# Attention and expert layers on one core: the scores of two key tiles merged in PSUM by a predicated copy before the bias is added

## The chip, the cores and the metric

The program runs on one core of one Trainium2 chip. The metric is the time of one execution on the device in microseconds (us). TensorE (PE) multiplies matrices and loads its weights through a queue of its own (PEld); VectorE (DVE), ScalarE (ACT) and GpSimd (POOL) do the rest; SyncE (SP) issues the loads and stores. PE writes its products to PSUM, six banks of which this kernel shares as `b`.

## The reference

```python
def _attn_ref(q, k, v):                      # 4 batches, 8 heads, 576 positions, 64 deep
    scores = scale * np.matmul(q, k.transpose(0, 1, 3, 2))
    rel = pos[:, None] - pos[None, :]
    bias = slopes[:, None, None] * (-np.abs(rel))[None, :, :]
    mask = (rel >= 0) & (rel < 128)
    scores = np.where(mask, scores + bias[None], -1000000000.0)
    attn = np.exp(scores - np.max(scores, axis=-1, keepdims=True))
    attn = attn / (np.sum(attn, axis=-1, keepdims=True) + 1e-09)
    return np.matmul(attn, v)

def _moe_ref(x, domain_probs, w1, w2):       # 2304 tokens, 512 wide, 4 experts, 1024 hidden
    for e in range(E):
        h = np.maximum(x @ w1[e], 0.0)
        out += p[:, e:e + 1] * (h @ w2[e])
```

A query sees itself and the 127 positions before it. So a tile of 128 queries needs two tiles of keys, its own and the one before, and of each pair of columns at the same offset exactly one is in the window: the own key where its offset is not above the query's, the earlier key where it is.

## The kernel before, in words

All arithmetic is 32-bit: a value that goes to PE is split into a high and a low part (tiles `kh`, `kl`, `w1h`, `w1l` and so on), and three products stand for one. The 2304 tokens are 18 tiles of 128 in seven blocks (`BLOCKS`): three of 256 tokens and four of 384. Attention for a block must be done before the expert layers (L923 first layer, L1111 second, L1001 a seven-product form for pairs of blocks) can use it. Attention is cut into units: one tile of 128 queries and one pair of heads. Block 0 (`plain`) has eight units and runs before anything else; block 1, also eight units, and the rest run among the expert products.

A planner (`Plan`) sets the order. Each piece of work is an `op` with the engines that may do it, a cost for each, a due time, the data that it reads and writes and the buffers that it holds; `Plan.order` goes through time, gives each op an engine and a buffer by these costs, and emits all instructions in that order. So a changed cost moves unrelated work too.

A unit (`unit`, L493) goes like this. PE writes the scores of both heads into one bank, up to 256 columns a head (L510 for block 0, L519 else). DVE adds the bias and takes the row's extreme (`least`, L555, one instruction a head). ACT takes exponentials with their sum (L573); the sum's reciprocal (L604) scales them (L612 on DVE or L620 on ACT); PE transposes them (L638); ACT or DVE split the result into high and low (L311, L313, L323) and PE multiplies with the values (L709). `pk` is the number of earlier keys that the tile has (0, 64 or 128: a sequence of 576 is four and a half tiles), `edge` is set where a sequence ends inside the tile.

The bias tile holds 256 columns a head: the same 128 numbers are loaded twice (L1178) and masked on POOL, one half for keys after the query, one for keys before (`seen`, L1164). From block 2 on (`FOLD`, L533) the two halves are folded after the bias: a minimum on DVE (L587) over the two 128-column halves, so that exponentials, scaling and transposes work on 128 columns. The transposed, split result is then parted again into own and earlier keys by two selections on POOL (`side`, L662). Tiles with `pk` of 64 fill the missing half with a memset (L551), tiles with an edge take a copy of the bias with a part overwritten (L544, L547). Block 1 has no fold: all stages run on 256 columns, four transposes a unit, and nothing for POOL to select.

Of the kernel before, what the change touches and what calls it, by code (L numbers as in the profile page):

```python
# [202 lines left out]
FOLD = 2  # L203

# [24 lines left out]
def attention_moe(  # L229
# [66 lines left out]
    bias = sb.tile([P, H, 2 * P], F32, tag="bias", name="bias")  # L296
# [117 lines left out]

    groups = {}
# [77 lines left out]
    def unit(u):  # L493
# [5 lines left out]
        edge = edge if edge < P else 0  # L499
        bk, s, t = Buf("b"), Buf("acc" if g.plain else "s"), Buf("t")  # L500
        sv = lambda: s[:, : 4 * P].rearrange("p (h n) -> p h n", h=2) if s.tag == "acc" else s.place
# [31 lines left out]
        fold = pk > 0 and g.nb >= FOLD  # L533
        o2, n2 = (P, P) if fold else (o, n)
# [3 lines left out]
        bkey = [("bias", g.hp)] if pk else [("bias", g.hp, 1)]  # L538
        bv = lambda: bias[:, hs, :]
        if edge:  # L540
            bb = Buf("x")
            b2 = lambda: bb[:].rearrange("p (h n) -> p h n", h=2)
            plan.op(
                {POOL: 0.75}, lambda e: nc.gpsimd.tensor_copy(b2(), bias[:, hs, :]), d - 1, [*bkey, "scores"], [bb], port=(POOL,)  # L544
            )
            plan.op(
                {POOL: 0.3}, lambda e: nc.gpsimd.memset(b2()[edge:, :, : P + edge], NEG), d - 1, [], [bb], port=()  # L547
            )
            bv, bkey = b2, [bb]
# [22 lines left out]
        def exponents(h):  # L572
            return lambda e: nc.scalar.activation(  # L573
                sv()[:, h, o2:],
                sv()[:, h, o2:],
# [6 lines left out]
        for h in range(2):  # L582
            plan.op({DVE: 0.15 + n / 960}, least(h), d + 0.3, [*bkey, bk], [(s, h), (t, h)])
        if fold:
            plan.op(
                {DVE: dve(2 * P)},
                lambda e: nc.vector.tensor_tensor(out=sv()[:, :, P:], in0=sv()[:, :, P:], in1=sv()[:, :, :P], op=ALU.min),  # L587
                d + 0.35,
                [(t, 0), (t, 1)],
                both,  # L590
                port=(DVE,),
            )
        for h in range(2):
            plan.op({ACT: 0.29 + n2 * 0.00087}, exponents(h), d + 0.4, [(t, h)], [(s, h), (t, 2 + h)])
# [15 lines left out]
        def weights_(e):  # L610
            if e == DVE:
                nc.vector.tensor_tensor(  # L612
                    out=sv()[:, :, o2:],
                    in0=sv()[:, :, o2:],
                    in1=t[:, 4:6, None].to_broadcast([P, 2, n2]),
# [3 lines left out]
            for h in range(2):  # L619
                nc.scalar.activation(sv()[:, h, o2:], sv()[:, h, o2:], AF.Copy, scale=t[:, 4 + h : 5 + h])  # L620

        plan.op({DVE: dve(2 * n2), ACT: 0.4 + n2 * 0.00174}, weights_, d + 0.7, [(t, 4)], both, port=(DVE,))
# [10 lines left out]
        tp = lambda: bk2[:].rearrange("p (h n) -> p h n", h=2)  # L633

        def transposed(e):
            for h in range(2):
                for c in (P,) if fold else (0, P)[2 - w // P :]:
                    nc.tensor.transpose(tp()[:, h, c : c + P], sv()[:, h, c : c + P], ident)  # L638

        tm = 2 if fold else 2 * w // P  # L640
# [3 lines left out]
        if g.plain:  # L644
            for h in range(2):
                cast(
                    lambda h=h: g.pt[h][:, c0 : c0 + w],
                    lambda h=h: tp()[:, h, 2 * P - w :],
# [6 lines left out]
        elif fold:  # L655
            hl = lambda: s[:].rearrange("p a b -> p (a b)").rearrange("p (x h n) -> p x h n", x=2, h=2)
            part = lambda x: hl()[:, x].bitcast(F32R)
            cast(lambda: part(0), lambda: tp()[:, :, P:], 2 * P, d + 0.9, [bk2], both, False)
            minus(lambda: part(1), lambda: tp()[:, :, P:], lambda: part(0), 2 * P, d + 1.0, [bk2], both, False)
# [14 lines left out]
        else:  # L674
            part = lambda x: pt[:, x, :, c0 : c0 + w]
            cast(lambda: part(0), lambda: tp()[:, :, 2 * P - w :], 2 * w, d + 0.9, [bk2], [(g.pt[0], i)], False)
            minus(
                lambda: part(1),
                lambda: tp()[:, :, 2 * P - w :],
                lambda: part(0),  # L680
                2 * w,
                d + 1.0,
                [bk2],
                [(g.pt[0], i)],
                False,
            )
# [475 lines left out]
    def seen(part, after):  # L1162

        return lambda e: nc.gpsimd.affine_select(  # L1164
            out=part,
            in_=part,
            pattern=[[0, 2], [1, P] if after else [-1, P]],
            base=0,
            channel_multiplier=-1 if after else 1,
            compare_op=ALU.is_gt if after else ALU.is_ge,  # L1170
            fill=NEG,
        )

# [145 lines left out]
```

## Time and profile before

| | |
|---|---|
| Runs of the kernel before | 903.31, 903.73 and 905.81 us; median 903.73 us |
| Span of the profiled execution, first to last instruction | 902.9 us |
| PE busy | 889.0 us, 98% |
| PEld, DVE, ACT, POOL busy | 805.3, 710.7, 449.9 and 371.3 us |
| DMA | 96.18 MB, 107 GB/s on average, 246 GB/s in the first fortieth of the span |

The profile is one execution; no time of its own is given for it apart from its span, which is 0.4 us below the fastest of the three runs and 0.8 us below their median. A busy engine is one with an instruction in work; matmuls overlap, so the distance from one start to the next tells more than their durations. A line number is a line of the kernel before; a helper's line (L311, L313, L323) stands for many uses, which are told apart by tile.

### The profile page before, as it was taken

What the parts mean: (1) busy time and instruction counts of PE and PEld (TensorE: products, weight loads), DVE (VectorE), ACT (ScalarE), POOL (GpSimd) and SP (SyncE); (2) the same over time, 40 slices, a digit from 0 to 9 for tenths busy, and PEclk for the clock granted to TensorE, in tenths of its full rate; (3) what the DMA queues carried; (4) which work ended last, traced back from release to release, by engine and by line L of the source; (5) the groups of instructions that cost most, each with busy time, mean ns of one, the idle gap of its engine ahead of it and who ended that gap; (6) DMA issues with size and microseconds to landing.
All of it is one profiled execution on the core that took longest, in us unless ns stands there. A gap on an engine that the chain in (4) does not pass through costs nothing.

```text
span 902.9 us, 14383 instructions
## 1 busy us (share of the span) xinstructions
PE 889.0 (98%) x5108; PEld 805.3 (89%) x5108; DVE 710.7 (79%) x1476; ACT 449.9 (50%) x1145; POOL 371.3 (41%) x348
## 2 busy tenths in 40 slices
PE   7899999999999999999999999999999999999998
PEld 5798999999999988999999998899898989989997
DVE  4888888687899899887887997677976767677765
ACT  4987454455556566765553344344333434344340
POOL 2656345253434467776525673213622222122100
PEclk9999999999999999999999999999999999999999
DMA  9766444243444345633111121212222121212001
GB/s 246 236 210 213 134 151 141 56 140 101 135 143 130 105 158 170 210 127 114 47 48 47 47 94 48 94 48 94 100 89 68 49 92 47 94 47 93 25 1 70
DMA packets 39959, 96.18 MB, mean 107 GB/s; under 512 B 3792, under 2 KB 17488, under 8 KB 39888
## 3 DMA queue, kind: packets, MB, share of 16 engines
q1 hardware_dynamic: 39888, 95.28, 32.6%
q8 instruction: 40, 0.66, 0.3%
q14 instruction: 31, 0.25, 0.1%
HBM read 90.54 MB, written 4.72 MB: 105 GB/s over the span
## 4 chain that ended last, share of the span: by engine, by line
PE 91%; DVE 6%; DMA 1%; ACT 1%; issue 1%; POOL 0%; DVEq 0%; POOLq 0%; ACTq 0%
PE b L1111 41%; PE b L923 22%; PE b L1001 18%; PE av L709 4%; PE b L519 3%; PE b L638 2%; DMA k<-in_qk 1%; PE b L510 1%; DVE w1l L323 1%; DMA w1r<-in_w 1%; DVE w2l L323 1%; DVE acc L1129 1%; DVE s L555 0%; DVE vs L323 0%; DVE x L736 0%
## 5 line engine op out<-in xcount | busy, mean ns | idle before, releaser
L1129 DVE SCALAR_TENSOR_TENSOR acc<-b,prob,acc 128x512 f32<-128x512 f32 (+1 forms) x229 | 169.8, 743 | 68.3 <-PE b L1111 67.5
L1111 PE MATMUL b<-w2h,rh 128*128 128x512 f32 x440 | 174.2, 396 | 0.0
L1111 PE MATMUL b<-w2h,rl 128*128 128x512 f32 x440 | 172.6, 392 | 0.4 <-DVE rl L951 0.4
L1111 PE MATMUL b<-w2l,rh 128*128 128x512 f32 x440 | 172.9, 393 | 0.0
L923 PE MATMUL b<-xh,w1h 128*128 128x256 f32 (+1 forms) x528 | 160.6, 304 | 1.3 <-ACT t L568 1.3
L923 PE MATMUL b<-xl,w1h 128*128 128x256 f32 (+1 forms) x528 | 157.0, 297 | 1.3 <-DVE xl L323 1.3
L923 PE MATMUL b<-xh,w1l 128*128 128x256 f32 (+1 forms) x528 | 157.0, 297 | 0.0
L323 POOL TENSOR_TENSOR w2l<-w2r,w2h 128x512 fp32r<-128x512 f32 x48 | 70.2, 1466 | 129.9 <-ACT w2h L311 116.3
L662 POOL TENSOR_SCALAR_AFFINE_SELECT pt<-s 128x512 fp32r<-128x512 f32 x104 | 67.9, 677 | 101.4 <-DVE s L323 79.1
L923 PEld LDWEIGHTS b<-xl,w1h 128*128 128x128 f32 x528 | 100.2, 190 | 3.7 <-DVE xl L323 1.7
L923 PEld LDWEIGHTS b<-xh,w1h 128*128 128x128 f32 x528 | 100.3, 190 | 3.5 <-ACT t L568 1.5
L944 ACT ACTIVATE rh<-b 128x256 fp32r<-128x256 f32 (+1 forms) x132 | 53.7, 407 | 96.9 <-PE b L923 92.1
L923 PEld LDWEIGHTS b<-xh,w1l 128*128 128x128 f32 x528 | 100.0, 189 | 0.0
L1111 PEld LDWEIGHTS b<-w2h,rl 128*128 128x128 f32 x440 | 82.6, 188 | 18.9 <-DVE rl L951 0.8
L1111 PEld LDWEIGHTS b<-w2h,rh 128*128 128x128 f32 x440 | 83.0, 189 | 10.6
L1111 PEld LDWEIGHTS b<-w2l,rh 128*128 128x128 f32 x440 | 83.0, 189 | 10.2
L951 DVE SCALAR_TENSOR_TENSOR rl<-b,rh 128x256 fp32r<-128x256 f32 (+1 forms) x132 | 60.2, 456 | 30.2 <-ACT rh L944 29.0
L323 POOL TENSOR_TENSOR w1l<-w1r,w1h 128x512 fp32r<-128x512 f32 x45 | 64.1, 1430 | 41.5 <-ACT w1h L311 17.9
L573 ACT ACTIVATE s<-s,t 128x128 f32<-128x128 f32 (+1 forms) x128 | 52.0, 408 | 47.7 <-DVE s L587 42.8
L1035 ACT ACTIVATE xh<-b 128x384 fp32r<-128x384 f32 x46 | 22.6, 491 | 92.3 <-DVE b L1020 85.4
L311 ACT ACTIVATE w2h<-w2r 128x512 fp32r<-128x512 f32 x109 | 64.5, 621 | 5.5 <-PE b L1111 4.5
L323 DVE TENSOR_TENSOR w2l<-w2r,w2h 128x512 fp32r<-128x512 f32 x72 | 62.5, 881 | 0.3 <-ACT w2h L311 0.2
(157 smaller groups left out, 1967.8 us busy)
## 6 DMA issues: line engine op xcount, KB each, us to landing
w1r<-in_w SPq DMA_DIRECT2D x60, 512.0 KB, 4.2
w2r<-in_w SPq DMA_DIRECT2D x60, 512.0 KB, 3.5
q<-in_q SPq DMA_DIRECT2D x16, 384.0 KB, 3.4
k<-in_k SPq DMA_DIRECT2D x12, 512.0 KB, 3.9
k<-in_k SPq DMA_DIRECT2D x12, 384.0 KB, 3.7
out<-acc SPq DMA_DIRECT2D x17, 256.0 KB, 2.1
v<-in_v SPq DMA_DIRECT2D x12, 256.0 KB, 2.9
v<-in_v SPq DMA_DIRECT2D x12, 192.0 KB, 3.4
```

Of the source, the lines that this page charges most:

```text
L311: nc.scalar.activation(o(), i(), AF.Copy)
L323: by[e].tensor_tensor(out=o(), in0=a(), in1=f(b()), op=ALU.subtract)
L519: nc.tensor.matmul(sc()[:, h, :n], g.qs[:, h, u.q0 : u.q0 + P], m[:, h, u.k0 : u.k0 + n], start=m is g.kh, stop=m is g.kl,)
L573: return lambda e: nc.scalar.activation(sv()[:, h, o2:], sv()[:, h, o2:], AF.Exp, bias=t[:, h : h + 1], scale=-1.0, accum_out=t[:, 2 + h : ...
L662: return lambda e: nc.gpsimd.affine_select(out=pt[:, :, :, c0 + own * P : c0 + own * P + P], in_=hl(), pattern=[[0, 4], [1, P] if own else ...
L709: nc.tensor.matmul(g.av[h][:, q0 : q0 + m], v2, g.pt[h][:, c : c + m] if g.plain else pt[:, x, h, c : c + m], start=not g.started[h], stop ...
L923: nc.tensor.matmul(bk[:, :n], a[0][:, kt, fs], b[:, kt, cols], start=kt == 0 and i == 0, stop=kt == KT - 1 and i == 2,)
L944: lambda e: nc.scalar.activation(h[:, :n], bk[:, :n], AF.Relu),
L951: lambda e: nc.vector.scalar_tensor_tensor(out=lo[:, :n], in0=bk[:, :n], scalar=0.0, in1=f(h[:, :n]), op0=ALU.max, op1=ALU.subtract,),
L1001: nc.tensor.matmul(bank[:, :n], x(k), y(k), start=new and k == 0 and i == 0, stop=k == 1 and i == 2, skip_group_check=True,)
L1111: nc.tensor.matmul(bk[:, cs], a[:, ns], b[1][:, fi, cs], start=half != 1 and fi == 0 and j == 0, stop=half != 0 and fi == 1 and j == 2, sk ...
L1129: nc.vector.scalar_tensor_tensor(out=o, in0=i_, scalar=p, in1=o, op0=ALU.mult, op1=ALU.add)
```

## The change

`FOLD` goes. Every unit outside block 0 with earlier keys is folded, so block 1 too, and the fold moves ahead of the bias: a predicated copy on DVE writes the earlier tile's scores over the own tile's in PSUM wherever a constant mask `after` says that the key is later than the query. The bias is then 128 columns a head, loaded once and unmasked. Where a mask is still needed (block 0, tiles with `pk` below 128, edges) POOL makes a masked copy of the bias for that unit in a buffer `x`. `least` works on 128 columns a head; the minimum and the memset are gone. The stages behind it and the selections are those of the fold before.

```diff
-FOLD = 2
...
-    bias = sb.tile([P, H, 2 * P], F32, tag="bias", name="bias")
+    bias = sb.tile([P, H, P], F32, tag="bias", name="bias")
+    after = sb.tile([P, 2, P], F32, tag="after", name="after")
...
+        fold = not g.plain
...
-        fold = pk > 0 and g.nb >= FOLD
...
+        if g.plain:
+            if u.first:
+                g.bb = Buf("x")
...
+            if pk:
+                plan.op({POOL: 0.45}, seen(lambda: b2()[:, :, :P], bv, True), d - 1, [bkey], [(bb, 0)], port=(POOL,))
+            else:
+                plan.op({POOL: 0.45}, seen(lambda: b2()[:, :, P:], bv, False), d - 1, [bkey], [(bb, 1)], port=(POOL,))
...
+        elif edge or pk < P:
+            bb = Buf("x")
...
-        if 0 < pk < P:
-            plan.op({POOL: 0.3, DVE: 0.28}, lambda e: by[e].memset(sv()[:, :, :o], -NEG if fold else 0.0), d, ["scores"], both, port=())
+        if fold and pk:
+            plan.op(
+                {DVE: 0.1 + 2 * pk / 960},
+                lambda e: nc.vector.copy_predicated(sc()[:, :, P:n], after[:, :, o:].bitcast(mybir.dt.uint32), sc()[:, :, :pk]),
+                d + 0.25,
+                ["after"],
+                [bk],
+            )
+        m = P if fold else n
+        f0 = n - m
...
         def least(h):
             return lambda e: nc.vector.tensor_tensor_reduce(
-                out=sv()[:, h, o:],
-                in0=sc()[:, h, :n],
-                in1=bv()[:, h, o:],
+                out=sv()[:, h, -m:],
+                in0=sc()[:, h, f0:n],
+                in1=bv()[:, h, :],
...
-        if fold:
-            plan.op(
-                {DVE: dve(2 * P)},
-                lambda e: nc.vector.tensor_tensor(out=sv()[:, :, P:], in0=sv()[:, :, P:], in1=sv()[:, :, :P], op=ALU.min),
...
-        for i, due in ((1, -37), (0, -33)):
...
+        load(
+            lambda hs=hs: bias[:, hs, :],
+            lambda hs=hs: bfd[:, hs, :],
+            131072,
+            -37 + 6 * hp,
```

The planner orders the whole program anew. Three places of that order are shown.

The first is SP's queue behind the first load of the program, up to the third load of keys and queries for block 0 (`k_63` the second time; `k_63` and `k_64` are the two buffers of keys and queries). Before:

```order
L304 DMA bias<-in_bias 128x2x128
L304 DMA v_65<-in_v 128x256
L304 DMA ident<-in_ident 128x128
L304 DMA bias<-in_bias 128x2x128
L304 DMA k_64<-in_qk 64x1024
L304 DMA bias<-in_bias 128x2x128
L304 DMA v_66<-in_v 128x256
L304 DMA bias<-in_bias 128x2x128 x3
L304 DMA dp<-in_dp 128x72
L304 DMA k_63<-in_qk 64x1024
```

Changed:

```order
L303 DMA bias<-in_bias 128x256
L303 DMA v_65<-in_v 128x256
L303 DMA ident<-in_ident 128x128
L303 DMA k_64<-in_qk 64x1024
L303 DMA bias<-in_bias 128x256
L303 DMA v_66<-in_v 128x256
L303 DMA bias<-in_bias 128x256
L303 DMA dp<-in_dp 128x72
L303 DMA bias<-in_bias 128x256
L303 DMA w1r_91<-in_w 128x1024
L303 DMA q_61<-in_q 128x2x256
L303 DMA k_63<-in_qk 64x1024
```

Two loads of bias fewer stand ahead of the third `k` (four against six), and the first load of weights and one of `q` have moved ahead of it.

The second is DVE's queue at one unit of a later block (`s_75` and `s_76` hold the unit's scores, `b_` are PSUM banks, `ISA` is the instruction of `least` and its read of the extreme into `t_`). Before:

```order
L555 ISA s_75,t_83<-b_126,bias 128x256
L555 ISA t_83 128x1
L951 SCALAR_TENSOR_TENSOR rl_107<-b_124,rh_103 128x256
L555 ISA s_75,t_83<-b_126,bias 128x256
L555 ISA t_83 128x1
L313 CAST s_77<-b_121 128x256
L323 TENSOR_TENSOR s_77<-b_121,s_77 128x256
L587 TENSOR_TENSOR s_75<-s_75 128x2x128
```

Changed:

```order
L586 COPY_PREDICATED b_125<-after,b_125 128x2x128
L312 CAST s_75<-b_122 128x256
L595 ISA s_76,t_81<-b_125,bias 128x128
L595 ISA t_81 128x1
L322 TENSOR_TENSOR s_75<-b_122,s_75 128x256
L595 ISA s_76,t_81<-b_125,bias 128x128
L595 ISA t_81 128x1
```

The fold has moved from behind the two instructions of `least` to ahead of them, and these have half the columns.

The third is POOL's queue while block 1's units run. Before, it holds only splits of weights, keys, queries and values:

```order
L323 TENSOR_TENSOR qs_67<-q_61,qs_67 64x2x256
L323 TENSOR_TENSOR vs_73<-v_65,vs_73 128x3x128
L323 TENSOR_TENSOR w1l_97<-w1r_91,w1h_95 128x512
L323 TENSOR_TENSOR w2l_102<-w2r_94,w2h_100 128x512
L323 TENSOR_TENSOR kl_72<-k_64,kh_70 128x2x384
L323 TENSOR_TENSOR w1l_98<-w1r_92,w1h_96 128x512
L323 TENSOR_TENSOR w2l_101<-w2r_93,w2h_99 128x512 x2
```

Changed:

```order
L322 TENSOR_TENSOR qs_67<-q_61,qs_67 64x2x256
L322 TENSOR_TENSOR vs_74<-v_66,vs_74 128x3x128
L705 AFFINE_SELECT pt<-s_75 128x4x128 x2
L322 TENSOR_TENSOR w2l_101<-w2r_93,w2h_99 128x512
L705 AFFINE_SELECT pt<-s_76 128x4x128 x2
L322 TENSOR_TENSOR w2l_101<-w2r_93,w2h_99 128x512
L322 TENSOR_TENSOR qs_68<-q_62,qs_68 64x2x256
L705 AFFINE_SELECT pt<-s_77 128x4x128 x2
L705 AFFINE_SELECT pt<-s_75 128x4x128 x2
```

Eight pairs of selections, one a unit of block 1, now stand between the splits.

## Rows read from the trace of the kernel before

**Rows 1.** The page: busy time by engine; the chain that ended last, by engine

```profile
PE 889.0 (98%) x5108; PEld 805.3 (89%) x5108; DVE 710.7 (79%) x1476; ACT 449.9 (50%) x1145; POOL 371.3 (41%) x348
PE 91%; DVE 6%; DMA 1%; ACT 1%; issue 1%; POOL 0%; DVEq 0%; POOLq 0%; ACTq 0%
```

**Rows 2.** Waits of PE, 34 us to the end: us in total, times, longest

```profile
PE b L923 <- DVE xl L323: 1.3, 2, 0.8
PE av L709 <- DVE x L736: 0.4, 1, 0.4
PE b L1111 <- DVE rl L951: 0.4, 1, 0.4
PE b L1001 <- DVE x L1078: 0.2, 1, 0.2
```

**Rows 3.** Waits of PE, first 34 us

```profile
PE b L510 <- DMA k<-in_qk: 5.8, 3, 4.6
PE b L923 <- ACT t L568: 1.3, 1, 1.3
PE av L709 <- ACT acc L311: 1.1, 1, 1.1
PE b L923 <- DVE xl L323: 0.8, 1, 0.8
```

**Rows 4.** Busy time by stretch: us, then PE, PEld, DVE, ACT, POOL

```profile
22.00:34.00 12.00, 8.70 (x55) 7.09 (x55) 11.30 (x35) 11.90 (x37) 6.19 (x5) 1.00 0.70 229
34.00:75.00 41.00, 41.00 (x292) 38.28 (x293) 33.74 (x83) 34.70 (x94) 28.57 (x20) 1.00 0.70 227
```

**Rows 5.** Timeline of PE at two units' transposes: start, us, instruction

```profile
76.14 0.60 PE L638 MATMUL b<-ident,s 128*128 128x128 f32 x4
76.49 0.36 PE L519 MATMUL b<-kh,qs 128*128 128x256 f32 x1
...
308.40 0.38 PE L638 MATMUL b<-ident,s 128*128 128x128 f32 x2
308.54 0.36 PE L519 MATMUL b<-kh,qs 128*128 128x256 f32 x1
```

**Rows 6.** Timeline of PE in block 0

```profile
12.23 1.22 PE L510 MATMUL b<-k 64*128 64x128 f32 x4 [0.49 <-DMA k<-in_qk]
...
19.52 0.71 PE L510 MATMUL b<-k 64*128 64x128 f32 x4
```

**Rows 7.** Timeline of POOL at the start: the masking of the bias, when each load landed

```profile
9.33 0.41 POOL L1164 TENSOR_SCALAR_AFFINE_SELECT bias<-bias 128x256 f32<-128x256 f32 x1 [0.45 <-DMA bias<-in_bias]
10.11 0.41 POOL L1164 TENSOR_SCALAR_AFFINE_SELECT bias<-bias 128x256 f32<-128x256 f32 x1 [0.37 <-DMA bias<-in_bias]
11.02 0.41 POOL L1164 TENSOR_SCALAR_AFFINE_SELECT bias<-bias 128x256 f32<-128x256 f32 x1 [0.50 <-DMA bias<-in_bias]
12.56 0.41 POOL L1164 TENSOR_SCALAR_AFFINE_SELECT bias<-bias 128x256 f32<-128x256 f32 x1 [1.14 <-DMA bias<-in_bias]
14.37 0.41 POOL L1164 TENSOR_SCALAR_AFFINE_SELECT bias<-bias 128x256 f32<-128x256 f32 x1 [1.40 <-DMA bias<-in_bias]
```

**Rows 8.** Groups of DVE by line and shape: busy us, mean ns, idle before

```profile
L555 DVE CUSTOM_DVE_ANT_0 s<-b,bias 128x256 f32<-128x256 f32 x88 | 34.5, 417 | 4.9 <-PE b L519 4.2 <-PE b L638 0.5
L587 DVE TENSOR_TENSOR s<-s 128x256 f32<-128x256 f32 x52 | 33.0, 639 | 0.3
L323 DVE TENSOR_TENSOR s<-b,s 128x256 fp32r<-128x256 f32 x52 | 21.7, 417 | 2.2 <-ACT s L311 1.8
L555 DVE CUSTOM_DVE_ANT_0 s<-b,x 128x256 f32<-128x256 f32 x16 | 6.2, 416 | 1.0 <-POOL x L547 1.0
L555 DVE CUSTOM_DVE_ANT_0 s<-b,bias 128x128 f32<-128x128 f32 x8 | 2.0, 280 | 0.0
```

**Rows 9.** Groups of POOL by line and shape

```profile
L323 POOL TENSOR_TENSOR w2l<-w2r,w2h 128x512 fp32r<-128x512 f32 x48 | 70.2, 1466 | 129.9 <-ACT w2h L311 116.3 <-DVE w2h L313 7.9 <-issue 5.3
L662 POOL TENSOR_SCALAR_AFFINE_SELECT pt<-s 128x512 fp32r<-128x512 f32 x104 | 67.9, 677 | 101.4 <-DVE s L323 79.1 <-DVE t L604 12.2 <-ACT rh L944 4.0
```

More of the change, by code (lines that the diff above doesn't have):

```diff
@@ L413, in attention_moe, with seen @@
             gs.append(g)
+    def seen(part, src, later):
+        return lambda e: nc.gpsimd.affine_select(
+            out=part(),
+            in_=src(),
+            pattern=[[0, 2], [1 if later else -1, part().shape[2]]],
+            base=0,
+            channel_multiplier=-1 if later else 1,
+            compare_op=ALU.is_gt if later else ALU.is_ge,
+            fill=NEG,
+        )
     groups = {}
@@ L529, in unit @@
         plan.op({PE: passes_ * mm(n)}, scores, d, qk, [bk, "scores"], [s], passes_ * mmc(n), late=late)
[L533 to L538 removed]
+        bkey = ("bias", g.hp)
         bv = lambda: bias[:, hs, :]
[L540 to L549 removed]
@@ L612, in weights_ @@
                 nc.vector.tensor_tensor(
-                    out=sv()[:, :, o2:],
-                    in0=sv()[:, :, o2:],
-                    in1=t[:, 4:6, None].to_broadcast([P, 2, n2]),
+                    out=sv()[:, :, -m:],
+                    in0=sv()[:, :, -m:],
+                    in1=t[:, 4:6, None].to_broadcast([P, 2, m]),
                     op=ALU.mult,
@@ L619, in weights_ @@
             for h in range(2):
-                nc.scalar.activation(sv()[:, h, o2:], sv()[:, h, o2:], AF.Copy, scale=t[:, 4 + h : 5 + h])
-        plan.op({DVE: dve(2 * n2), ACT: 0.4 + n2 * 0.00174}, weights_, d + 0.7, [(t, 4)], both, port=(DVE,))
+                nc.scalar.activation(sv()[:, h, -m:], sv()[:, h, -m:], AF.Copy, scale=t[:, 4 + h : 5 + h])
+        plan.op({DVE: dve(2 * m), ACT: 0.4 + m * 0.00174}, weights_, d + 0.7, [(t, 4)], both, port=(DVE,))
         i = u.q0 // P
@@ L632, in unit @@
         bk2 = Buf("b")
-        tp = lambda: bk2[:].rearrange("p (h n) -> p h n", h=2)
+        tp = lambda: bk2[:, : 2 * m].rearrange("p (h n) -> p h n", h=2)
         def transposed(e):
             for h in range(2):
-                for c in (P,) if fold else (0, P)[2 - w // P :]:
-                    nc.tensor.transpose(tp()[:, h, c : c + P], sv()[:, h, c : c + P], ident)
-        tm = 2 if fold else 2 * w // P
+                for c in range(0, m, P):
+                    nc.tensor.transpose(tp()[:, h, c : c + P], sv()[:, h, sv().shape[2] - m + c : sv().shape[2] - m + c + P], ident)
+        tm = 2 * m // P
         plan.op(
@@ L1159, in output @@
                 )
[L1162 to L1172, printed above, removed]
     for hp in range(NPAIR):
         hs = slice(2 * hp, 2 * hp + 2)
-        for i, due in ((1, -37), (0, -33)):
-            cs = slice(i * P, i * P + P)
-            load(
-                lambda hs=hs, cs=cs: bias[:, hs, cs],
-                lambda hs=hs: bfd[:, hs, :],
-                131072,
-                due + 6 * hp,
-                [],
-                [("bias", hp, i)],
-            )
-            plan.op(
-                {POOL: 0.36},
-                seen(bias[:, hs, cs], i == 0),
-                due + 0.5 + 6 * hp,
-                [("bias", hp, 1)],
-                [("bias", hp, i), ("bias", hp)],
-            )
+        load(
[3 more added lines that the diff above has]
+            -37 + 6 * hp,
+            [],
+            [("bias", hp)],
+        )
+    plan.op({POOL: 0.3}, lambda e: nc.gpsimd.memset(after, 1.0), -2, [], ["after"], port=())
+    plan.op(
+        {POOL: 0.45},
+        lambda e: nc.gpsimd.affine_select(
+            out=after,
+            in_=after,
+            pattern=[[0, 2], [1, P]],
+            base=0,
+            channel_multiplier=-1,
+            compare_op=ALU.is_gt,
+            fill=0.0,
+        ),
+        -2,
+        [],
+        ["after"],
+    )
     load(lambda: ident, lambda: idd, 65536, -36, [], ["ident"])
```

73 lines of the change are left out of this document (44 added, 29 removed).

## The prediction

> **What bounds the kernel now.** I read the page first: PE is busy 98% of the span and holds 91% of the chain that ended last, DVE 6% [rows 1]. Busy time of PE is no proof, since matmuls overlap, so I next read who PE waited for. From 34 us to the end, 869 us, it waited 2.3 us in all, and each time for DVE [rows 2]. In the first 34 us it waited 5.8 us for loads of keys and queries (4.6 of them for one load) and 3.2 us for ACT and DVE [rows 3]. Then the busy times by stretch: between 22 and 34 us ACT is busy 11.90 and DVE 11.30 of 12 us, so there these two set when PE goes on; from 34 to 75 us PE is busy without a gap, and POOL 28.57 of 41 us [rows 4]. So a change counts in three places only: PE's own work, the first 34 us, and the 2.3 us of waits behind. Work saved on DVE, ACT or POOL elsewhere gives nothing by itself.
>
> **The sum.** It starts from the span of 902.9 us and is then carried to the median of the runs, 903.73 us, which stands 0.8 us above it; I treat that as what lies around the span and add it unchanged.
>
> 1. *PE's work.* Block 1's eight units transpose two tiles instead of four; scores and value products keep their shapes, and the later blocks were folded already. A unit of four transposes takes 0.35 us from its start to that of the next instruction, a unit of two 0.14 us, and both times the next instruction has the same form [rows 5]. So 8 x 0.21 = 1.7 us go from an engine that has no gap there. This is the one term that nothing hides: **-1.7 us**.
>
> 2. *DVE.* Removed: the minimum, 52 x, 33.0 us busy. Halved: 104 instructions of the bias at 256 columns, 34.5 + 6.2 = 40.7 us busy; at 128 columns one is 2.0 / 8 = 0.25 us busy, so 104 cost 26.0 and 14.7 go [rows 8]. Added: 52 predicated copies of 256 elements (44 units of later blocks with 128 earlier keys, and block 1's eight) and eight of 128. No row shows this instruction. The nearest is the subtraction of a PSUM and an SBUF operand of the same 256 elements, 417 ns; from below I take 280 ns, the 128-column row, and from above twice the nearest, 0.83 us, should the old contents of the bank be read as a stream of its own [rows 8]. I take 417 ns, as the operands match, and 280 ns for the small ones: 52 x 0.417 + 8 x 0.28 = 23.9 us. DVE is then relieved by 33.0 + 14.7 - 23.9 = 24 us; at 0.28 by some 31, at 0.83 (0.42 for the small ones) by 1. None of these makes it busier. All of this lies beside PE, save where PE waits for DVE: of the 2.3 us [rows 2] I take a quarter, **-0.5 us**, because the planner lays out all work anew and puts other DVE work close to its due time. The minimum's row is itself remarkable: 639 ns for 256 elements against 417 ns for an instruction with one operand in PSUM [rows 8]; the new copy has that operand form, not the minimum's.
>
> [...]
>
> 3. *Start.* Four of eight bias loads go. Three of them landed 0.78 and 0.91 us apart in the old queue (9.33, 10.11, 11.02), so each holds it for about 0.8 us; the loads that stay write one run a partition where they wrote two. The second load of keys and queries stands behind one bias load instead of two and should land some 0.8 us sooner; PE waited 0.7 us there (5.8 - 4.6 - 0.49, rows 3 and 6). Against that the third one has lost two bias loads ahead of it (-1.7 us) but has a load of weights (512 KB) and one of `q` (256 KB) in front. A weight and a bias load together, 640 KB, took 14.37 - 12.56 = 1.81 us [rows 7], so 768 KB take 2.2 us: it lands 0.5 us later. The planner has put the transposes of an earlier unit ahead of it on PE, so this should be covered. The early weights let ACT and DVE split them while they still had room, but between 22 and 34 us both are full [rows 4], and the amount of work that stands before block 0's last values on either is about what it was. A further half microsecond may come or go with the place of a product: the same four matmuls took 1.22 us at 12.23 and 0.71 us at 19.52 [rows 6]. Bounds: -2.2 us (the two later waits for keys, 1.2 us, and a third of the 3.2 us of waits for ACT and DVE) and +2.2 us (the moved loads fully in the way). I take **-0.5 us**, the share of the second load. POOL's masks of the bias are still eight in block 0, 0.41 us each [rows 7], now in a buffer a unit pair and ahead of the unit; the two POOL instructions that make the mask run while POOL had nothing to do.
>
> [...]
>
> 4. *POOL.* Block 1 adds 16 selections at 677 ns [rows 9], 10.8 us, between 34 and some 80 us. On top of 28.57 of 41 us [rows 4] that would leave POOL almost no room; but the order shows that splits have moved away from it there, and I count its load as up by about four tenths of that. Covered by PE's work, price nothing, unless a pair comes late (below). The new masks for tiles with an edge or 64 earlier keys replace a copy and memsets of like size; none is on PE's path.
>
> 5. *ACT.* Exponentials, scaling and splits of block 1 at half width: less work beside PE's. Nothing.
>
> Sum: 902.9 - 1.7 - 0.5 - 0.5 = 900.2 us for the span, and 903.73 - 2.7 = **901.0 us** for the run.
>
> **The rivals.**
>
> *The start gives back what the transposes give.* The third load of keys and queries comes 2.2 us later and PE stands for it: 903.7 - 1.7 - 0.5 + 2.2 = 903.7 us. For it: PE did wait 0.49 us for that load before [rows 6] and 768 KB are now ahead. Against it: the two bias loads that are gone, and PE's new order.
>
> *The waits go.* Lighter DVE and earlier data remove all 2.3 us of rows 2 and the 2.2 us that I allowed at the start: 903.7 - 1.7 - 2.3 - 2.2 = 897.5 us. For it: every wait behind 34 us is for DVE. Against it: the planner uses each gap for the next split.
>
> *Slower: POOL becomes the bound in block 1.* The values of a block-1 unit now need two selections on POOL (1.35 us a pair) behind whatever split stands ahead, 1.47 us [rows 9], where before DVE or ACT wrote them directly. If PE reaches the value products one split too early in four of eight units, it stands 4 x 1.47 = 5.9 us: 901.0 + 5.9 = 906.9 us. It decides once POOL's load between 34 and 75 us nears the 41 us: 28.57 + 10.8 = 39.4 if no split had moved. Against it: splits did move, and the same pairs run in later blocks without a wait of PE for POOL [rows 2].
>
> **How the numbers follow.** The forecast has 0.5, its own range 899.5 to 902.5 us; the start's loss 0.2, the end of the waits 0.17, POOL 0.13. About 0.3%, or 2.7 us, is what a measurement of this kernel can tell from no change, so the line for faster lies at 901.0 us: half of the forecast (0.25) and the second rival, with a little of the first, give 0.44 for faster, the rest of the first and the forecast 0.43 for no difference, POOL 0.13 for slower. The range 897.5 to 906.0 us leaves out half of the end-of-waits case and most of POOL's, no more than 2 in 10.
>
> **What would show it.** Right: 16 transposes fewer for the `s` tiles; a row of predicated copies near 417 ns and none of the minimum; PE waiting from 34 us on for under 2 us; its first long stretch without a gap beginning within a microsecond of 34 us. Wrong: PE waiting for POOL's selections between 34 and 80 us (slower), a wait for the third load of keys and queries above 1 us (no difference), or no wait left behind 34 us (faster than I say). If the predicated copy costs 0.8 us and the time is still near 901, DVE was hidden as I say; if the time then rises, DVE mattered more than its waits show.

## The result and the profile after

The changed kernel takes 910.12 us (median of 5 runs), the kernel before 903.73 in the same job: ratio 1.0062, 95% interval [1.0043, 1.0081]. The forecast was 901.0, the range ended at 906.0, and the chance given to "slower" was 0.13.

The profiled execution of after took 910.32 us with a span of 908.6, against 902.9 before. The first part of its page, busy time by engine, to be laid beside [rows 1]:

```profile
PE 890.2 (98%) x5092; PEld 807.0 (89%) x5092; DVE 703.3 (77%) x1483; ACT 448.2 (49%) x1144; POOL 388.4 (43%) x391
```

PE has its 16 transposes fewer, DVE and ACT have less work and POOL 17.1 us more. By busy time nothing got tighter. Who PE waited for, from 34 us to the end and then in the first 34 us (us in total, times, longest), against [rows 2, 3]:

```profile
PE b L669 <- ACT s L651: 2.3, 2, 1.6
PE b L1031 <- DVE x L1108: 1.9, 1, 1.9
PE b L953 <- DVE xh L312: 1.0, 1, 1.0
PE b L532 <- DVE kl L322: 0.7, 1, 0.7
PE b L953 <- DVE xl L322: 0.5, 1, 0.5
...
PE b L523 <- DMA k<-in_qk: 5.1, 1, 5.1
PE av L739 <- ACT acc L310: 1.7, 1, 1.7
PE b L669 <- DVE t L610: 1.1, 1, 1.1
PE b L669 <- DVE acc L643: 0.8, 2, 0.7
```

Behind 34 us the waits rose from 2.3 to 6.4 us, and the start's total is about what it was (8.7 against 9.0). The waits of before are gone, others stand at 34, 83, 91, 197 and 531 us, and none is for POOL. The second half of the loss is in PE's granted clock, the third figure from the end in the busy times by stretch (us, then PE, PEld, DVE, ACT, POOL, clock):

```profile
33.00:35.00 2.00, 0.55 (x3) 0.19 (x1) 1.91 (x4) 0.00 (x0) 0.00 (x0) 1.00 0.92 285
35.00:37.00 2.00, 1.95 (x11) 1.95 (x12) 1.94 (x9) 1.17 (x6) 0.06 (x1) 0.64 0.97 369
37.00:39.00 2.00, 2.00 (x11) 2.00 (x11) 0.81 (x7) 2.00 (x9) 1.92 (x2) 0.50 0.43 154
39.00:41.00 2.00, 2.00 (x16) 1.87 (x15) 2.00 (x9) 1.56 (x6) 1.14 (x1) 1.00 0.55 120
531.00:533.00 2.00, 0.81 (x4) 0.33 (x2) 1.86 (x1) 1.06 (x2) 1.89 (x2) 1.00 0.00 0
533.00:535.00 2.00, 1.31 (x5) 1.30 (x6) 2.00 (x5) 1.27 (x3) 0.00 (x0) 0.73 0.00 0
535.00:537.00 2.00, 2.00 (x8) 2.00 (x7) 1.46 (x4) 1.45 (x4) 1.62 (x2) 0.50 0.00 0
537.00:539.00 2.00, 2.00 (x12) 1.91 (x11) 2.00 (x3) 1.11 (x3) 1.18 (x1) 0.92 0.49 129
```

After the waits at 34 us, and after the one at 531 us, PE's granted clock is 0.50 for some 3 us: products of 256 columns start 0.21 us apart at 36 us, and 0.12 us at 39 us, where the clock is at 1.00 again. The missing parts of these rows, taken as an estimate of the time lost, are 2 x (0.36 + 0.50) and 2 x (0.27 + 0.50 + 0.08): 1.7 us each. In the profile of before the same stretch behind block 0 has 1.00 throughout. The account of the span: waits +4.1 and -0.3, clock +3.4, transposes -1.7, together 5.5 of the 5.7 us.

What makes one of these waits shows at 531 us. The timeline of after, first DVE's rows and then POOL's (start, us, instruction):

```profile
530.20 0.55 DVE L1050 TENSOR_TENSOR b<-b,s 128x384 f32<-128x384 f32 x1
531.14 2.03 DVE L885 TENSOR_TENSOR w1r<-w1r 128x256 f32<-128x256 f32 x1 [0.40 <-POOL q L885]
533.09 0.54 DVE L1108 TENSOR_TENSOR x<-b,s 128x384 f32<-128x384 f32 x1
...
530.37 0.74 POOL L885 TENSOR_TENSOR q<-w1r 128x256 f32<-128x256 f32 x1 [0.62 <-DMA w1r<-in_w]
531.07 1.82 POOL L885 TENSOR_TENSOR k<-k,xl 128x768 f32<-128x768 f32 x1
```

The sum `x` (L1108), which PE needs, stands behind a sum of weights that is not urgent. That one waited for POOL, began 0.07 us after a long POOL instruction, and took 2.03 us; the 24 of its line and shape that write `q` take 0.48 us in the mean, and the four others that write `w1r` 0.81. The planner books such instructions of DVE and POOL one behind the other (`port` in `Plan.order`) and had put this one ahead of POOL's; POOL did not wait for it. Why it took so long was not shown; the rows have its 2.03 us beside POOL's 1.82.

So the first theory was: the instructions are sound, and it is the new order that loses (**order**). Its rivals: block 1's fold crowds POOL and DVE (**block 1**); the copy itself; the start, where a weight load and a `q` load now stand ahead of the third load of keys and queries.

### The profile page after: what moved, and what is told of

Read it like the earlier page. It is cut to its first block, busy times and chain, and to the rows that moved or that the text cites. A ratio compares the mean times of both kernels' runs of the same rounds, so it can differ in the third digit from the quotient of the medians.

```text
span 908.6 us, 14398 instructions
## 1 busy us (share of the span) xinstructions
PE 890.2 (98%) x5092; PEld 807.0 (89%) x5092; DVE 703.3 (77%) x1483; ACT 448.2 (49%) x1144; POOL 388.4 (43%) x391
## 4 chain that ended last, share of the span: by engine, by line
PE 91%; DVE 5%; ACT 2%; DMA 1%; issue 1%; POOL 0%; SPq 0%; DVEq 0%; POOLq 0%
PE b L1141 42%; PE b L953 22%; PE b L1031 18%; PE av L739 4%; PE b L532 3%; PE b L669 2%; PE b L523 1%; DVE w2l L322 1%; DVE w1l L322 1%; DVE acc L1159 1%; DVE kl L322 1%; DMA k<-in_qk 0%; DMA w1r<-in_w 0%; DVE k L885 0%; ACT acc L613 0%
## 5 line engine op out<-in xcount | busy, mean ns | idle before, releaser
L322 POOL TENSOR_TENSOR w2l<-w2r,w2h 128x512 fp32r<-128x512 f32 x44 | 64.7, 1472 | 127.7 <-ACT w2h L310 121.0
L705 POOL TENSOR_SCALAR_AFFINE_SELECT pt<-s 128x512 fp32r<-128x512 f32 x120 | 78.2, 676 | 83.3 <-DVE s L322 57.6
L613 ACT ACTIVATE s<-s,t 128x128 f32<-128x128 f32 x128 | 50.5, 396 | 57.2 <-DVE t L595 56.7
L885 POOL TENSOR_TENSOR q<-w1r 128x256 f32<-128x256 f32 x22 | 18.3, 833 | 103.8 <-DMA w1r<-in_w 91.8
```

Source lines behind the costliest of these rows:

```text
L322: by[e].tensor_tensor(out=o(), in0=a(), in1=f(b()), op=ALU.subtract)
L613: return lambda e: nc.scalar.activation(sv()[:, h, -m:], sv()[:, h, -m:], AF.Exp, bias=t[:, h : h + 1], scale=-1.0, accum_out=t[:, 2 + h : ...
L705: return lambda e: nc.gpsimd.affine_select(out=pt[:, :, :, c0 + own * P : c0 + own * P + P], in_=hl(), pattern=[[0, 4], [1, P] if own else ...
```

## The experiments

One execution doesn't tell much here: single runs of the kernel before lie between 903.3 and 910.7 us, and their median between 903.7 and 907.5 us from job to job. So the verdicts go by ratios to before over 5 rounds, each to the runs of before in its own job; a difference in microseconds between two jobs says less.

**First round: parts taken out, and places mended.** All parts in orders of the planner's own, except for the named moves.

Only block 1's fold, in the old way:

```diff
-FOLD = 2
+FOLD = 1
```

> The kernel before with block 1 folded too, in the old way (the minimum of the two tiles behind the bias, masks in the bias, old start): of the change only the second block's fold. If the fold of block 1 costs the time (more selections on POOL beside DVE's operations), it reaches 907 to 910 and the waits for DVE appear between 75 and 200 us. If the new order alone is at fault, the fold itself is worth its 1.7 us of transposes, and the time is 902.0 give or take what this plan's own order does (899 to 907), with its waits at places of its own.

914.4 us, ratio 1.0096 [1.0072, 1.0119]. PE waits 3.5 us for `w1l`, 2.0 for `kl` and 0.5 for `qs`, all between 58 and 88 us, sooner than expected: block 1 fits, and beyond the 910 expected.

The change without block 1's fold:

```diff
-        fold = not g.plain
+        fold = g.nb > 1
...
-        if g.plain:
+        if g.nb < 2:
...
-        elif not pk:
+        elif not fold:
```

> The changed kernel with block 1 as it was (no fold, both tiles weighed and transposed, its bias masked in a buffer of its own): the predicated copy stays in blocks 2 to 6. If the fold of block 1 costs the time, it comes back to 904 to 905. If the copy in place of the minimum costs it, it stays at 909 to 912. If it is the order, the time is anywhere in 901 to 910, and the PE waits of over 1 us lie at other places than 91 and 531 us of the changed kernel.

913.4 us, 1.0091 [1.0063, 1.0119]. (The four units of tile 9, which have no tile behind them, take the branch with selections here, eight selections more, so that tile's output is another; the last run of the second round leaves this out.) Between 75 and 120 us no wait is left, as block 1 says; but the waits came back elsewhere, 2.7 us for `x` L1108 and 1.7 us for the third load of keys and queries. Not 904: the order counts too.

One operation moved to POOL, by its number in the plan:

```diff
+    moved = {2464: (POOL, 525.06)}
+    for o in line:
+        o.eng, o.start = moved.get(o.n, (o.eng, o.start))
```

> The changed kernel, one operation moved from DVE to POOL: the w1r sum of 256 columns at 531 us, which took 2.03 us on DVE beside POOL's 768 columns and stood ahead of what PE waited for. If the order is the cause, PE's wait of 1.88 us there is gone, and with it the half rate that follows (some 1.6 us): 906.8, between 906.0 and 908.5. If the waits are only a sign of DVE or POOL being too full, the wait turns up within 20 us of it and the time stays at 909.5 to 910.5.

911.4 us, 1.0056 [1.0032, 1.0080]; no gain that can be told from the changed kernel's 1.0062. The wait at 531 us is gone, and another of 1.4 us for the same `x`, one product group on, stands at 550 us. Up to 531 us the program is that of after, and yet in this execution PE waited 2.3 us more for loads at the start, 7.4 instead of 5.1 us in all:

```profile
PE b L523 <- DMA k<-in_qk: 7.4, 2, 4.5
```

The second of these waits, 2.9 us, is for the third load, behind the 768 KB; the products that use it begin at 15.70 us. In after's profile they begin at 13.34 us and this wait is nil. In the profiles of the run above and of the next one, with the same queue, it is 1.7 and 1.2 us.

Four places mended at once:

```diff
-    moved = {2464: (POOL, 525.06)}
+    moved = {134: (ACT, 27.83), 133: (DVE, 28.05), 135: (DVE, 28.38), 187: (DVE, 28.71), 1003: (DVE, 30.64),
+        322: (DVE, 74.4), 371: (DVE, 83.26), 2464: (POOL, 525.06)}
```

> The changed kernel with the operations at four places in another order and nothing else changed: at the end of block 0 one xh cast to ACT, the last xl differences ahead of a kl and a w2l on DVE; at 82 us kl ahead of an accumulation; at 91 us the qs difference behind the reciprocal and an rl; the operation at 531 us on POOL. If the order is the cause: minus 0.9 at the start, 0.7 at 82 us, 1.3 to 2.8 at 91 us with the half rate behind it, 3.4 at 531 us, so 903.5, between 902 and 905.5, with the same instructions as the changed kernel at 910. If the instructions are the cause (copy, selections, the new start), 908.5 to 910.5.

916.4 us, 1.0122 [1.0093, 1.0151], but inconclusive: my list put a `kl` difference of block 1 behind the next load into the buffer that it reads, so part of block 1's scores comes from other keys, and PE waits 4.6 us for that difference. At 82 and 91 us the waits I mended went and others came, 1.2 us for `w1h` and 1.0 for an accumulation. (The lower clock that was expected to go with the wait at 91 us isn't in after's profile: there it stands behind the waits at 34 and 531 us only.)

**Second round: nudged plans.**

```diff
-EXTRA = 0.03
+EXTRA = 0.025
```

> The kernel before with one constant of the planner changed, the margin behind every wait from 0.03 to 0.025 us: the same instructions in another order. If the order decides, it is over 2 us away from the kernel before, in either direction, with waits of PE at places of their own: 901 to 912. If the instructions decide, 903.5 to 906.

918.45 us, 1.0156 [1.0128, 1.0184]: the same instructions as before, 14.5 us slower. PE's longest waits behind 34 us, in a profile of the slowest of its six executions (923.06 us):

```profile
PE av L709 <- DVE pt L323: 2.9, 2, 2.3
PE b L923 <- DVE w1l L323: 2.7, 1, 2.7
PE b L1111 <- DVE rl L951: 1.8, 2, 1.2
PE b L923 <- ACT t L568: 1.3, 1, 1.3
PE b L638 <- ACT s L620: 0.8, 1, 0.8
PE b L1001 <- DVE x L1078: 0.8, 1, 0.8
```

They are of the kind of after's: mostly something that was late on DVE, somewhere else. So the order of the kernel before is a good one, and a neighbour that the planner makes can be far worse; how good it is among many was not tried.

The same edit in the changed kernel:

> The changed kernel with the same constant changed in the same way. If the order decides, it is over 2 us away from 910, and no longer has waits at 91 and 531 us: 903 to 916. If the instructions decide (block 1's fold, the copy, the start), 909 to 911.5, and the loss between 75 and 120 us stays near 3 us in this order too.

914.3 us, 1.0109 [1.0085, 1.0133]; waits of 1.3, 1.1 and 0.9 us between 75 and 120 us, none at 531 us. This fits order and block 1 alike.

The start mended, by making the first `w1`, `w2` and `q` loads follow the first score products in the plan:

```diff
-            load(lambda r=r: r[:], lambda src=src: src[e, fp], 524288, due - 10 + 4 * i, [], [r, f"load{i}"])
+            load(lambda r=r: r[:], lambda src=src: src[e, fp], 524288, due - 10 + 4 * i, ["first"], [r, f"load{i}"])
...
```

> The changed kernel, with the loads of w1, w2 and the later q held back in the plan until the third k load of block 0 can go: on SP's queue the third k stands ahead of the first w1r again, as in the kernel before. If that load's way through the queue is the start's loss, PE waits at most 0.6 us for the third k (0, 1.2, 1.7 and 2.9 us in the four profiles with the changed kernel's queue) and the time falls by 1 to 2 us, to 908.5; as the whole plan is another, 905 to 912. If the start is not it, that wait is as before and the time 910.

915.4 us, 1.0119 [1.0096, 1.0142]. The wait for the third load is 0.6 us, as said; the rest of the new plan loses far more (2.7 us for `acc`, 2.2 for `rl`).

The same, and block 1 without the fold:

```diff
-        fold = not g.plain
+        fold = g.nb > 1
...
-        elif not pk:
+        elif not fold or not pk:
```

> The edit above, and block 1 without the fold (both tiles weighed and transposed). If the fold of block 1 crowds DVE and POOL, PE loses under 0.5 us between 75 and 120 us (3.2 us in the changed kernel), and with the start mended the time is 904.5, between 901 and 908. If the plan's order alone decides, the time is anywhere between 901 and 913 and the loss between 75 and 120 us need not be small.

911.7 us, 1.0081 [1.0058, 1.0104]. No wait between 75 and 120 us (where the changed kernel's waits are 0.7 and 1.6 us, 2.3 and not 3.2), 0.4 us for the third load, and still 5.0 us of waits in sum from 34 us on. Of the six new orders of the planner's own in these two rounds none had a median below 911 us: a part can't be judged while each edit deals out a new order.

**Third round: one order held.** The planner's choice is replaced by a list, which keeps every operation common to both kernels on the engine and in the place that it has in the kernel before. An operation whose buffer isn't free yet goes in as soon as it is.

```diff
-        for o in plan.order():
+        for o in plan.follow(LINE):
```

The whole change with its list:

> The changed kernel, all its instructions, in the order of the kernel before: the planner's choice is replaced by a written list, which puts every operation that both kernels have on the engine and in the place that it had before; the copy stands ahead of its reduces, block 1's selections behind their differences, the masks ahead of their unit. TensorE's rows are those of before but for the 16 transposes. If the new order is the cause and the instructions are worth what the sum of the prediction said, the time is 901.0, between 899.5 and 904, 6 to 9 us under the changed kernel with the same instructions. If the instructions are the cause (POOL's selections in block 1, the copy, the bias masks at the start), it is 907 to 911 in this order too, and PE waits between 34 and 120 us.

911.97 us, 1.0041 [1.0024, 1.0059].

With `fold = g.nb > 1` as above, and its own list by the same rule:

> The same, without block 1's fold (its two tiles weighed and transposed as before): copy, single bias and masks by unit alone, and TensorE's rows word for word those of before. If the order is the cause: 902.7, between 901.5 and 905, as the 1.7 us of transposes are not saved. If block 1's fold is what costs, this is at 903 to 904 and the run above 4 us or more slower. If the copy or the start costs, both are at 907 or more.

905.9 us, 0.9990 [0.9974, 1.0006].

The kernel before with `FOLD = 1`, and the list:

> The kernel before with block 1 folded in the old way, in the order of before (it was 914.4 in its own plan's order). If the order is the cause: 902.0, between 901 and 905. If the fold of block 1 crowds DVE and POOL: 907 to 914, with PE waits between 50 and 95 us.

916.4 us, 1.0092 [1.0073, 1.0111].

This parts the theories. In one order, the copy and the single bias (with four loads fewer) show no cost and no gain: 0.9990, or 0.9 us less with 1.5 us either way. The other part of the new start, a weight load and a `q` load ahead of the third load of keys and queries, isn't in this order and isn't tested here. Block 1's fold makes the whole loss that is left, 4.6 us by the ratios (0.0051 of 907), 6.1 by the medians. Done in the old way, by a minimum, it costs 8 us (0.0092 of 907). Order as the only cause has fallen: with before's order kept, the whole change is still slow. PE's waits from 34 us to 125 us, of the whole change, of the same without block 1's fold, and of the old fold:

```profile
PE av L791 <- POOL pt L757: 4.1, 5, 1.1
PE b L1005 <- DVE xh L364: 1.3, 1, 1.3
PE b L1005 <- DVE xl L374: 1.1, 1, 1.1
```

```profile
PE b L1005 <- ACT t L660: 1.3, 1, 1.3
PE b L1005 <- DVE xl L374: 1.2, 2, 0.8
```

```profile
PE av L761 <- POOL pt L714: 6.4, 7, 1.4
PE b L975 <- DVE xh L365: 2.7, 1, 2.7
PE b L975 <- DVE xl L375: 0.8, 1, 0.8
PE b L690 <- DVE rl L1003: 0.4, 1, 0.4
```

Here it is POOL's selections by name (L757, L714; the line numbers are those of the lengthened files): five waits at four of block 1's eight units, and seven at five units with the old fold. The timeline of the whole change in the old order, POOL, then the difference on DVE that feeds the selections, then PE:

```profile
45.11 1.47 POOL L374 TENSOR_TENSOR vs<-v,vs 128x384 fp32r<-128x384 f32 x1
46.55 1.29 POOL L374 TENSOR_TENSOR w1l<-w1r,w1h 128x512 fp32r<-128x512 f32 x1
47.80 1.67 POOL L757 TENSOR_SCALAR_AFFINE_SELECT pt<-s 128x512 fp32r<-128x512 f32 x2
```

```profile
46.40 0.42 DVE L374 TENSOR_TENSOR s<-b,s 128x256 fp32r<-128x256 f32 x1
```

```profile
47.83 0.28 PE L1005 MATMUL b<-xh,w1l 128*128 128x256 f32 x1
48.94 1.25 PE L791 MATMUL av<-pt,vs 128*128 128x256 f32 x8 [0.83 <-POOL pt L757]
```

The input is there at 46.82, the selections begin at 47.80 behind a split of weights, and take 1.67 us; PE stands from 48.1 to 48.9. POOL's busy time from 34 to 120 us is the fifth figure in the next rows, of before, of the change without block 1's fold, and of the whole change, the last two in the old order:

```profile
34.00:120.00 86.00, 85.49 (x589) 78.97 (x590) 73.40 (x172) 60.54 (x165) 47.64 (x42) 1.00 0.58 188
```

```profile
34.00:120.00 86.00, 83.74 (x573) 77.08 (x574) 73.98 (x175) 61.56 (x168) 53.65 (x52) 1.00 0.57 187
```

```profile
34.00:120.00 86.00, 79.94 (x527) 72.40 (x528) 71.88 (x172) 55.37 (x158) 57.72 (x59) 0.98 0.57 185
```

Two thirds busy is not full, and without the fold POOL is busy almost as long, 53.65 us, and PE doesn't wait for it; at 47.80 us what counts is that a pair meets a split that has just begun. Of the 5.2 us between the spans of the last two (910.1 and 904.9), the waits for POOL make 4.1; PE's clock is at 0.97, 0.50 and 0.68 between 35 and 41 us and costs 1.7, by the same estimate as above, where it stays at 1.00 without the fold; the transposes take off 1.7; the last 1.1 us are not traced to single places. The clock falls before PE waits for any selection. In 10 of 12 executions with the fold and 6 of 12 without it the mean clock is below 1.000, so how much of this 1.7 us the fold brings stays open.

One thing more moves the spans, and it is no part of the change. The kernel before and the change without block 1's fold have PE's instructions in the same order here, and yet the same eight products of values take 1.57 us in the one profile and 2.93 in the other:

```profile
21.81 1.57 PE L709 MATMUL av<-acc,v 128*128 128x256 f32 x8
```

```profile
22.79 2.93 PE L791 MATMUL av<-acc,v 128*128 128x256 f32 x8
```

In both PE begins at about half its later pace: before has 2.93 us for eight such products too, at 16.42 us (the clock column prints 1.00 in both stretches). It goes over to the later pace at 19 us in before, and between 25.5 and 27.5 us in the other, which ends 2.0 us later (spans of 902.9 and 904.9 us). From 20 to 34 us the other has PE busy for 13.18 us with 61 matmuls and the whole change for 12.94 us with 61, before for 10.70 us with 66. So the two of this round can be compared with each other; with before by span they can't.

**Fourth round: queue or length of the chain?** In the list, a `w1l`, a `w2l` and another `w1l` go behind the selections on POOL, a `w1l` and an accumulation behind the differences on DVE. The list is shown in part, by names and numbers of operations:

```diff
-[... w1l 1016, side 172, side 173 ...]
+[... side 172, side 173, w1l 1016 ...]
```

> The changed kernel in the old order, five operations moved so that block 1's selections go earlier: on POOL a w1l, a w2l and another w1l difference behind the selections that waited behind them (they started 1.0, 1.4 and 0.8 us after their input was there), on DVE a w1l difference and an accumulation behind the two differences that feed the selections at 85 and 89 us. If the place in POOL's queue makes the waits, PE's waits for pt fall from 4.1 to under 1.5 us and the time by 3 to 4.5 us, to 908.3 (907 to 909.5). If it is the length of the chain, or POOL and DVE are simply full, the waits stay or PE waits for w1l and w2l in their place: 911 to 912.5.

910.6 us, 1.0035 [1.0019, 1.0051]. Waits for `pt` fall from 4.1 to 2.4 us at three units, not under 1.5, and 0.4 us for a `kl` and 0.3 for an `rl` came in. Two of the three stand at units that had none before. By medians the gain is 1.4 us, between the two expectations; by ratios, 1.0041 and 1.0035, it can't be told from none.

Then PE's products of values of four units behind the next groups of its other work, on top:

```diff
-[... values 174, scores 205, products 1286 ...]
+[... scores 205, products 1286, values 174 ...]
```

> The same, and TensorE's products of values of four units moved behind the next one or two groups of its other work, so that each has 1 to 1.5 us more. If the length of the chain makes the waits, and this is all, PE waits under 0.5 us for pt, and the time is 904.5 (902.5 to 906.5): the fold's 1.7 us of transposes come out against the 905.9 of the run without it. If DVE and POOL are too full in this stretch, PE then waits for xl, w1l or w2l between 60 and 100 us, and the time is 907 to 911.

909.07 us, 1.0032 [1.0015, 1.0049]. `pt` 1.8 us at three units, again two of them units without a wait in the first list. So each edit takes away waits, as both the queue and the chain would have it, and neither ends them. That the time fell with them isn't shown: 1.0041 and 1.0032 lie within each other's intervals. By the middle of the ratios and by the medians alike, less than half of the fold's cost is given back.

**Fifth round: the end of block 0.** The last `xh` casts and `xl` differences of block 0 go ahead of a `w1l` and a `vs` on DVE and two exponentials on ACT; in the change without block 1's fold:

```diff
-[... least 149, exponents 150, 151, w1l 980, vs 143, xh 134, xh 132, least 160, xl 133, xl 135 ...]
+[... least 149, xh 132, xh 134, xl 133, xl 135, exponents 150, 151, w1l 980, vs 143, least 160 ...]
```

> The change without block 1's fold in the old order (905.9), and the last xh casts and xl differences of block 0 moved ahead of a w1l difference and a vs cast on DVE and of two exponentials on ACT. If these waits make the loss and bring the clock down, PE waits under 1 us there, the clock stays at 1.00, and the time falls by 1.2 to 2.5 us, to 904.0 (903 to 905). If not, something else waits in their place: 905.5 to 906.5.

905.96 us, 0.9992 [0.9975, 1.0009]. The two waits of 2.1 us shrink to one of 0.46, as said, but 0.6 us of others follow within 6 us and the time is the same. (In this profile PE goes over to its later pace at 19 us already, waits 1.8 instead of 0.5 us for the last `acc` of block 0, and 1.8 us for a sum `x` far behind; so the two profiles can't be laid side by side in more than this.)

The same four moves on top of the fourth round's:

> The whole change in the old order with selections ahead and products of values later (909.1), and the same four moves. If the waits at the end of block 0 and the clock behind them are a loss of their own: minus 1.5 to 3.5 us, 906.5 (905.5 to 908). The distance to the run above then is what block 1's fold costs at best care: 2.5 us, with its 1.7 us of transposes saved already in it. If the fold alone is at fault: 908.5 to 909.5.

909.8 us, 1.0046 [1.0028, 1.0064]: no gain; PE now waits 1.6 us for a `kl` at 52 us.

The same four moves in the kernel before:

> The kernel before with the same four moves and nothing else: 1.2 to 2.5 us under before in the same job if the waits count for themselves, and then as fast as the first of these three within 1 us, which would say that the copy and the single bias are worth nothing here. No change if the waits are hidden by something behind them.

904.5 us, 0.9993 [0.9977, 1.0009] of before: the same. So taking these waits away gave nothing beyond the 1.5 us that the intervals leave open, and no worth of the copy and the single bias shows in either direction (0.9992 with them, 0.9993 without). No version beat the kernel before; the change without block 1's fold, in the old order, can't be told from it.

## Why the prediction was wrong

**Two steps failed: step 4, which priced block 1's selections at nothing, and the stall term of step 2, which took the planner's new order as free.**

**Step 4, POOL.** Sixteen selections at 677 ns, 10.8 us, was nearly right: in the old order the whole run has 120 of them in 79.8 us, 688 ns each in the mean, where before has 104 in 67.9 us [rows 9]; that is 11.9 us more. "Covered by PE's work, price nothing" was not: PE waited 4.1 us at four units, and the fold of block 1 cost 4.6 us in all, its saved transposes already in it. The rival with chance 0.13, POOL becoming the bound in block 1, had the mechanism, the place and nearly the price: a pair behind a split in four of eight units, 5.9 us on top. But it had them for an order that the changed kernel doesn't have, so that its 906.9 us lies nearer the measured 910.1 than the forecast does is luck. The two reasons against it did not hold. That later blocks run such pairs without a wait said nothing of block 1, whose values PE asks for where POOL was 70% busy already [rows 4]. That splits had moved away from POOL in the new order was true (26.8 us busy from 34 to 75 us in the changed kernel, 28.6 before), but PE then waited for other work: 0.7 us for a `kl` difference on DVE at 83 us, and 1.6 us at 91 us for a scaling on ACT, whose reciprocal stood on DVE behind a difference of 1.58 us.

**The new order, in step 2's stall term.** I let the planner's new layout cost nothing but a share of the waits: -0.5 us, of 2.3. In the changed kernel the waits behind 34 us came to 6.4 us, and PE's clock, at 0.50 behind two of them, lost an estimated 3.4 us. The nudge of before (+1.56%) shows that a layout can cost 14.5 us with no instruction changed. Without block 1's fold, an order of the planner's own gives 1.0081 and the old one 0.9990. The two causes do not add: the fold in the old order makes 1.0041, a new order without the fold 1.0081, and both together, the changed kernel, 1.0062. How its 6.4 us are divided between them can't be said. What is shown is that a new order alone can cost this much, and the whole change in the old order two thirds of it.

**Step 1, PE's work.** The count is right, 5092 against 5108, and the 1.7 us are in every sum above. They are less than what PE loses by the fold's selections.

**Step 2, DVE.** The copy was taken at 417 ns by its operand form and takes 420; the small one, taken at 280, takes 285:

```profile
L586 DVE COPY_PREDICATED b<-after,b 128x256 f32<-128x256 uint32 x52 | 21.9, 420 | 7.2 <-PE b L532 6.9
L586 DVE COPY_PREDICATED b<-after,b 128x128 f32<-128x128 uint32 x8 | 2.3, 285 | 0.0
```

The relief was put at 24 us, and the instructions that were exchanged do give 23 (33.0 us of minima and 14.6 at `least`, against 24.2 of copies). But DVE's busy time fell by 7.4, as other work grew: 24 casts of `w1h` at 745 ns instead of 23 at 502, eight casts of `s` more, the sum that took 2.03 us above. In the old order without block 1's fold it fell by 16.2. A worth in time doesn't show: 0.9990 [0.9974, 1.0006] with it, which has room for the -0.5 us and for nothing. Where PE waited for DVE in the traces above, it was for the place of one instruction.

**Step 3, the start.** Forecast -0.5 us with bounds of 2.2 both ways. In the old order, with the third load ahead of the weights again, the four loads less show no gain. In the changed kernel's queue the third load is the weak place I had named, and PE's wait for it is 0 to 2.9 us from one execution to another, where I had put it as covered. The four matmuls that took 1.22 us at 12.23 and 0.71 at 19.52 [rows 6] were not a matter of a product's place: they stand before and behind PE's change of pace at 19 us. That change comes some 7 to 9 us later in the profiles of the change without block 1's fold (in the old order) and of the last run. The first of these has PE's instructions in before's order and a span 2.0 us longer, more than the half microsecond that I had allowed.

**Prices of waits.** I priced each at its length. Twice in the changed kernel a wait of 1 to 2 us was followed by an estimated 1.7 us of lost clock (0.50 for some 3 us), as much again.

**What would show it.** Of the signs I named, PE's waits behind 34 us came out at 6.4 instead of under 2 us, and the first gapless stretch began at 35.1 us instead of 33.9, just beyond the microsecond allowed; waits for POOL's selections between 34 and 80 us came in the old order only. The signs for being right in the parts came true: 16 transposes fewer, copies near 417 ns and no minimum.

## What to carry to other kernels

An order made by a planner is part of the kernel: an edit that makes it plan anew gives up the order that was measured, so price a new order by its own spread (nudge a constant that changes no instruction), and judge an edit's instructions with the old order held. A step that puts two more instructions of a shared engine between two PE steps is not free because that engine has room on average: look for what it stands behind when PE comes to it. Where PE is 98% busy, as here, 16 us less on DVE gave nothing that could be measured, and 1.7 us less of PE's own work was outweighed by 4.1 us of waits for the selections that came in its place.

## What the runs showed of the hardware that was not expected

- PE's granted clock fell to 0.50 for some 3 us after 1.5 us of waits at 34 us and 1.9 us at 531 us in after, and stayed at 1.00 after 2.1 us of waits at the same place in before and in the change without block 1's fold (in the old order). What decides it was not tried.
- PE's first 18 to 19 us in before, in after, in the fourth round's second run and in the fifth round's first two, and its first 26 to 28 in the change without block 1's fold (in the old order) and in the last run, went at about half the later pace: the same eight products took 2.93 and 1.57 us. The same order of PE's instructions came out 2.0 us longer with the later change of pace (904.9 against 902.9 us). What sets the moment was not tried.
- A DVE sum of 256 columns with both operands in SBUF took 2.03 us beside a POOL instruction of 1.82 us, where 24 others of its line and shape took 0.48 us in the mean; the predicated copy of as many, its data in PSUM, took 420 ns in the mean.
- When a load is there varies by more than the transposes are worth: with the same queue ahead of it, PE waited 0, 1.2, 1.7 and 2.9 us for the third load of keys and queries in four profiles. Two of these (0 and 2.9) are of programs that are alike up to 531 us.
